# Results in a used-up operand, an earlier operand load, and four moved steps in an attention and squared-ReLU kernel

## The chip, the cores and the metric

The kernel runs on one core of one Trainium2 chip. The metric is device time in microseconds (us). The engines are named as in the profile: PE is TensorE (PEld its weight load), DVE is VectorE, ACT is ScalarE, POOL is GpSimd and SP is SyncE. SP and ACT issue the DMAs here; a "q" behind an engine's name (SPq, ACTq) marks its sequencer.

## The reference

Attention in which a query sees only keys of its own cluster, then a feed-forward block with a squared ReLU. There are 4 batches, 8 heads, 768 positions and 64 elements to a head; d_model is 512 and d_ff 2048. Everything is float32.

```
q_assign = argmax(normalized q . normalized centroids)      # 16 clusters to a head
k_assign = argmax(normalized k . normalized centroids)
scores   = where(q_assign == k_assign, q @ k.T / 8, -1e9)
x        = softmax(scores) @ v                              # (3072, 512)
h        = x @ w_in                                         # (3072, 2048)
out      = max(h, 0)**2 @ w_out                             # (3072, 512)
```

## The kernel before

**Attention.** The loop over `p` takes the 16 pairs of heads (`NG`), four to a batch. A pair has nine tiles of scores, keys along the partitions: six of the first 512 queries and three of the other 256. `tile_of(p, i)` does one: matmuls of mask rows (`mask`, L450) and of keys and queries (`score`, L441) into one PSUM tile of a pool of three, then the exponential on ACT (L457). DVE adds the exponentials up (`total`, L460), PE multiplies them with v (`times_v`, L475), and ACT copies the result to `xT` (L484). Transposed q and k come by a DMA transpose (`turn_words`, `qkT`). `logits` (L329) are products with the centroids, of a later pair, into the pool of score tiles; `number` turns them on DVE into mask rows, which come back by way of DRAM (`far`, `rows`).

The sums of the exponentials: `add_up` (L494) sums over partitions on PE into half of a score tile, `invert` (L503 to L509) transposes and inverts them on DVE and stores them in DRAM, `spread` (L516) loads them broadcast, and `finish` (L526) multiplies a pair's `xT` with them in two DVE operations. All of pair p-1 but `add_up` happens in pass p; the last pair's is done inside the first up stage.

**Feed-forward.** The batches go in the order 1, 2, 3, 0 (`FEED`; n counts them). Each has an up stage (times w_in, squares) and a down stage (times w_out). The products are done by Winograd's form of Strassen's scheme: seven products of half-size blocks instead of eight, with sums of blocks made ahead and results added up behind. `x_sums` makes four sums of the input on DVE (L538), one at each `next`; `w_sums` makes those of w_in on POOL. An up stage has eight groups (`F2`). A group's seven products (L767) go into PSUM banks, which rotate among six; ACT copies the first (L730), DVE adds the others (L724, L538), ACT and DVE take the squares. In the first up stage DVE also rounds the blocks of w_out that are still being loaded (`Rounding.between`, L145 to L153, three a group in six groups) and makes sums of w_out (`w_out_sum`). What follows a group is in `Rounding.behind(i)`: after i = 0 the last pair's `add_up`, `invert` and `spread`; after i = 2 its `finish` and the store of x of batch 3 to DRAM (`x_far`, L1184).

**The down stages.** Two thirds of a batch's rows (`TWO`, 256 columns of g) go through its own down stage with the scheme applied twice. The last thirds (`THIRD`) of two batches are kept in DRAM (`g_far`) and done together: the stages of n = 1 and n = 3 have fourteen units (of, j), `of` 0 for the batch itself and 1 for the two thirds, j the outer product; the stage of n = 2 has seven. A unit (`Down.run`) has seven inner products (L956) into the banks `one` and `two`; ACT copies the first (L1089); `parts` makes the sums of the next unit's left operand; `combine`, a generator in two halves, adds up the unit before (L833) and lists finished quarters of the output; `store` issues these on ACT's queue at the next unit (L1071). The order of the units is

```
(0,1) (0,4) (1,4) (1,1) (0,5) (1,5) (0,7) (1,7) (0,6) (1,6) (0,2) (1,2) (0,3) (1,3)
```

`load_right(j)` (L915) loads four sums of w_out for the next j, `load_left(j)` (L994) the thirds from `g_far` in four DMAs, and `LATER` says after which unit (1, j) which left operand is loaded. The results of a stage stand in spare places: g's own last third (`third`), the tiles of the input's sums (`x_t1`, `x_t2`, `x_t4`) and the output pool. Left operand 3 of `of` = 1 is loaded into the last third of the half h = 1 of g, where results 21 and 22 stand until they are stored. Left operand 4 of `of` = 0 is `g[:, 8:16, 1, 0:256]`, used only in the second unit.

The order on each engine is the order in which the code issues (`manual_schedule`), but for the first down stage, which a planner orders. DMAs take turns on eight completion semaphores. At the end all engines read a flag (L1222) and branch past a general path (L1235).

Of the kernel before, what the change touches and what calls it, by code (L numbers as in the profile page):

```python
# [8 lines left out]
F32 = mybir.dt.float32  # L9
# [9 lines left out]
P = 128  # L19
# [6 lines left out]
def kernel(  # L26
# [432 lines left out]
    def add(eng, out, a, b):  # L459
        eng.tensor_tensor(out=out, in0=a, in1=b, op=ALU.add)  # L460
# [51 lines left out]
    def spread(pair):  # L512
        far = reciprocals.pop(pair)
        rb = endp.tile([P, 2, 32, NBL], F32, name="rb")
        for e in range(2):
            nc.sync.dma_start(  # L516
                rb[D * e : D * (e + 1)].rearrange("p g i b -> p (g i b)"),
                far[e].rearrange("i b -> (i b)").partition_broadcast(D),
            )
        spread_out[pair] = rb  # L520

    def finish(pair):
        b, hp = divmod(pair, HP)
        x = x_of(b)[:, hp].rearrange("p (g b i) -> p g b i", g=2, b=NBL)
        for g in range(2):
            nc.vector.scalar_tensor_tensor(  # L526
                out=x[:, g], in0=x[:, g], scalar=UP,
                in1=spread_out[pair][:, g].rearrange("p i b -> p b i"),
                op0=ALU.mult, op1=ALU.mult,
            )  # L530
        spread_out.pop(pair)
# [32 lines left out]
    def tile_of(pair, i):  # L564
        begin(i)
        for j in range(len(spots(i))):
            mask(pair, i, j, True)
            score(pair, i, j, False)
        exponential(i)
# [21 lines left out]

    first_sums = []
    x_early, w_early = x_sums(FEED[0]), []
    for p in range(NG):
        if p == 0:
            load_qk(3)
            load_ahead(0)
        if p == HP + 1:
            nc.sync.dma_start(x_far[FEED[3]], xT.pop(FEED[3]))
        if p:  # L600
            invert(p - 1)
            turn_words(p + 2)
            spread(p - 1)
        if 2 < p + 1 < NG:
            turn_logits(p + 1)
            number(p + 1)
        load_v(p + 1)
        if p:
            load_ahead(p - 1)


        if p == 0:
            for i in range(2):
                turn(1, i, (V, M)[i])
                score(p, i, 0, True)
            turn_onehot()
            for t in rows_of:
                nc.vector.memset(t, 0.0)
            turn(1, 2, V)
            for i in range(NB):  # L620
                if i == 2:
                    begin(i)
                    score(p, i, 0, True)
                mask(p, i, 0, False)
                exponential(i)
        else:
            for i in range(NB):
                tile_of(p, i)
        total[p] = endp.tile([P, 2, S], F32, name="total")
        first, last = total[p][:, :, 0:QA], total[p][:, :, QA:S]  # L630
        add(nc.vector, first, ex[0], ex[1])
        if p < 2:
            logits(p + 1, begin("ls"))
            turn_logits(p + 1)
            number(p + 1)
        add(nc.vector, first, first, ex[2])
        for i in range(NB, NCH):
            tile_of(p, i)
            add(nc.vector, first, first, ex[i])
        if p == 0:  # L640
            for i in range(2):
                split_words(2, i, nc.scalar)
            turn_words(2)
        else:
            split_words(p + 3, 0)


        for i in range(NCH, NCH + NB):
            tile_of(p, i)
        part = accp.tile([P, 2, 512], F32, name="part")  # L650
        add(nc.vector, part, ex[NCH], ex[NCH + 1])
        add(nc.vector, part, part, ex[NCH + 2])
        add(nc.vector, last, part[:, :, 0:QB], part[:, :, QB : 2 * QB])
        if p:
            finish(p - 1)
            round_2(p - 1)
            round_3(p - 1)
        if p == 0:
            split_words(3, 0)
        split_words(p + 3, 1)  # L660
        load_qk(p + 4, (nc.scalar, nc.scalar))
        round_1(p)


        for i in range(NCH):
            times_v(p, i, V)
        evict(p, 0, V)
        for i in range(NCH, NCH + NB):
            times_v(p, i, M)
        raw_v.pop(p)  # L670
        if p + 1 < NG:
            bank = begin("ls")
            if 2 < p + 2:
                if p + 2 < NG:
                    logits(p + 2, bank)
            add_up(p, bank[:, 1])
        evict(p, NCH, M)
        for d in (qkT, ohT):
            d.pop(p)
        if p >= NG - 2:  # L680
            for _ in range(2):
                if (found := next(x_early)) is not None:
                    first_sums.append(found)
            w_early.append(w_sums(len(w_early)))
    att.close()

# [272 lines left out]

    LATER = {1: 7, 5: 6, 7: 2, 2: 3}
    LOADS = ({1: (0,), 2: (1,), 3: (2,), 4: (3,)}, {9: (0,), 10: (1, 2), 12: (3,)})

    class Down:
# [55 lines left out]
        def find_results(self):  # L1021
            def four(t):
                return t.rearrange("p (i n) -> p i n", i=4)

            def tile(pool, tag):
                return four(pool.tile([P, 4 * P], F32, name="c", tag=tag))

            third = [self.g[:, F4 * i : F4 * (i + 1), 1, THIRD] for i in range(3)]
            if self.n % 2:
                self.c = [  # L1030
                    {11: tile(tp, "x_t2"), 21: third[0], 22: third[2]},
                    {11: tile(tp, "x_t4"), 21: tile(tp, "x_t1"), 22: third[1]},
                ]
                self.extra = xp.tile([P, 3, F2, P], F32, name="extra", tag="x1")
            else:
                self.c = [dict(zip((11, 22, 21), third))]
            for c in self.c:
                c[12] = tile(outp, "osb")


        def combine(self, of, j, one, two, copied):
            c = self.c[of]
            r = c[{1: 11, 4: 21, 5: 12, 7: 22}[j]] if j in (1, 4, 5, 7) else four_r
            plus(r[:, 0:2], two[:, 0:2], copied.unsqueeze(1).to_broadcast([P, 2, P]))
            plus(r[:, 2], two[:, 2], r[:, 1])
            plus(r[:, 1:4:2], two[:, 3].unsqueeze(1).to_broadcast([P, 2, P]), r[:, 1:3])
            yield
            if j in (2, 3):
                to = c[{2: 11, 3: 12}[j]]
                plus(to, to, r)  # L1050
                plus(to[:, 1:3], one[:, 1:3], to[:, 1:3])
            else:
                plus(r[:, 1:3], one[:, 1:3], r[:, 1:3])
            if j == 7:
                sub(c[21], c[22], c[21])
            elif j == 6:
                plus(r, c[11], r)
                for to in (21, 12):
                    plus(c[to], c[to], r)
                plus(c[22], c[22], c[12])  # L1060
            for to in {6: (21, 22), 2: (11,), 3: (12,)}.get(j, ()):
                self.stores.append((of, to))

        def store(self, queues=(nc.scalar, nc.scalar)):
            for of, to in self.stores:
                h, m = divmod(to, 10)
                h, m = h - 1, m - 1
                cols = slice(M2 * m, M2 * (m + 1))
                for i in range(2):
                    b, block = (FEED[self.n - 1 + i], 2) if of else (self.b, i)  # L1070
                    queues[i].dma_start(  # L1071
                        out_view[b, NB * h + block][:, cols].rearrange("p (m n) -> p m n", m=2),
                        self.c[of][to][:, 2 * i : 2 * i + 2],
                    )
            self.stores = []

        def run(self):
# [3 lines left out]
            for u, (of, j) in enumerate(self.units):  # L1081
# [14 lines left out]
                if waiting:  # L1096
                    next(waiting)
                sub(x[0][1], x[0][1], s[:, 1])
                times(one[:, 1], x[0][1], y[1][1])
                if u + 1 < len(self.units):  # L1100
                    if (k := self.units[u + 1][1]) != j:
                        load_right(k)
# [13 lines left out]
                        self.load_left(5)  # L1116
                if waiting:
                    next(waiting, None)
                waiting = self.combine(of, j, one, two, copied)
                to_end = len(self.units) - 1 - u  # L1120
                for kk in LOADS[self.n % 2].get(u, ()):
                    load_x(self.n + 1, kk)
# [3 lines left out]
                    sum_x(self.n + 1, 2)  # L1126
            list(waiting)
            sum_x(self.n + 1, 1)
            self.store((nc.sync, nc.scalar) if self.n == B - 1 else (nc.scalar, nc.scalar))


    flag = const.tile([P, 1], I32, name="flag")
# [15 lines left out]
    class Rounding:  # L1148
# [27 lines left out]
        def behind(self, i):  # L1176
            nonlocal wtp, spare_tile, four_r
            if i == 0:
                add_up(NG - 1, bank_tile(TB))
                invert(NG - 1)  # L1180
                spread(NG - 1)
            if i == 2:
                finish(NG - 1)
                nc.sync.dma_start(x_far[FEED[2]], xT.pop(FEED[2]))  # L1184
            if i == 5:
# [238 lines left out]
```

## Time and profile before

| | us |
|---|---|
| median of 3 runs | 891.62 |
| lowest and highest | 891.22, 892.13 |
| profiled execution, its own time | 892.71 |
| its span, first to last instruction | 890.8 |

| engine | busy us | share of the span |
|---|---|---|
| PE | 877.4 | 98% |
| PEld | 584.9 | 66% |
| DVE | 703.6 | 79% |
| ACT | 389.9 | 44% |
| POOL | 146.1 | 16% |

The granted TensorE clock was 0.998 over the span. In a line of the timeline the first number is the start in us, the second the time taken by the x instructions of the line, and brackets hold the idle time of the engine before it and what ended that. In a list of waits the numbers are the total in us, how many, and the longest. In an answer on one source line the numbers behind the count are the shortest, median and longest duration in ns, and then the first and last start in us.

### The profile page before, as it was taken

The page shows a single profiled execution, that of the slowest core. Times are in us where ns is not written, and L with a number is a line of the kernel's source. Part 1 is how long each engine was busy: PE and PEld are TensorE (multiplying, and loading weights), DVE is VectorE, ACT ScalarE, POOL GpSimd, SP SyncE. Part 2 cuts the span into 40 slices and gives each one's busy share as a digit, 9 for nine tenths or more (in the row PEclk, how much of TensorE's full clock was granted, in tenths as well). Part 3 has the DMA queues.
Part 4 walks back from the last instruction along what each step waited for, and adds up shares of the span by engine and source line. Part 5 has one row for each costly group of instructions (what it writes and reads, how often), then busy time and mean ns, then how long its engine had stood idle before and what let it go on. Part 6 is the DMA issues. An engine that isn't in the chain of part 4 may idle for free.

```text
span 890.8 us, 14588 instructions
## 1 busy us (share of the span) xinstructions
PE 877.4 (98%) x5379; PEld 584.9 (66%) x5379; DVE 703.6 (79%) x1271; ACT 389.9 (44%) x621; POOL 146.1 (16%) x168
## 2 busy tenths in 40 slices
PE   9999999999999999999999999999999999999995
PEld 6444444444444555568855599996558975579995
DVE  6798888888888989999756686778568786586794
ACT  5877667777666657740045410003452025430000
POOL 0000100000000247720222200013320052300000
PEclk9999999999999999999999999999999999999999
DMA  7767787767754235326701165573113741127553
GB/s 249 180 182 207 217 246 193 197 178 214 211 148 115 85 142 173 129 67 232 282 33 48 41 187 188 162 240 104 51 53 124 227 148 48 41 92 240 159 151 121
DMA packets 165729, 136.04 MB, mean 153 GB/s; under 512 B 58794, under 2 KB 139282, under 8 KB 165394
## 3 DMA queue, kind: packets, MB, share of 16 engines
q1 hardware_dynamic: 149634, 119.78, 45.1%
q10 hardware_dynamic: 16016, 15.24, 5.4%
q8 instruction: 45, 0.74, 0.3%
q14 instruction: 34, 0.28, 0.1%
HBM read 82.10 MB, written 41.89 MB: 139 GB/s over the span
## 4 chain that ended last, share of the span: by engine, by line
PE 86%; DVE 8%; DMA 4%; issue 2%; ACT 1%; ACTq 0%; DVEq 0%; SPq 0%
PE bank L767 30%; PE bank L956 19%; PE sc L441 12%; PE av_a L475 8%; PE bank L848 5%; PE av_b L475 4%; PE sc L450 3%; DMA g<-g_far 1%; PE sc L329 1%; PE sc L494 1%; DMA qkT<-words 1%; DVE spare L833 1%; DVE g L724 1%; DVE c L833 1%; DVE g L538 1%
## 5 line engine op out<-in xcount | busy, mean ns | idle before, releaser
L457 ACT ACTIVATE ex<-sc 128x1024 f32<-128x1024 f32 x144 | 144.2, 1025 | 38.7 <-PE sc L441 32.0
L724 DVE TENSOR_TENSOR g<-bank,g 128x384 f32<-128x384 f32 x192 | 102.5, 552 | 71.8 <-PE bank L767 64.0
L441 PE MATMUL sc<-qkT 64*128 64x512 f32 (+1 forms) x768 | 150.5, 484 | 0.0
L743 ACT ACTIVATE g<-g 128x384 f32<-128x384 f32 x122 | 63.3, 519 | 102.0 <-DVE g L724 97.9
L767 PE MATMUL bank<-xT,w_s 128*128 128x384 f32 x256 | 93.2, 487 | 0.9 <-DVE g L724 0.9
L441 PEld LDWEIGHTS sc<-qkT 64*128 64x128 f32 x768 | 65.9, 188 | 41.9 <-issue 30.1
L767 PE MATMUL bank<-xT,w_in 128*128 128x384 f32 x256 | 93.2, 487 | 0.0
L767 PE MATMUL bank<-x_t,w_s 128*128 128x384 f32 x256 | 93.0, 486 | 0.0
L1089 ACT COPY spare<-bank 128x128 f32<-128x128 f32 x35 | 9.2, 263 | 189.7 <-PE bank L956 171.7
L475 PE MATMUL av_a<-ex,v_raw 128*64 128x512 f32 x384 | 85.9, 596 | 0.0
L460 DVE TENSOR_TENSOR total<-total,ex 128x1024 f32<-128x1024 f32 x64 | 78.7, 1229 | 6.5
L558 POOL TENSOR_TENSOR w_s<-w_in 128x256 f32<-128x256 f32 x32 | 26.0, 811 | 317.7 <-PE bank L956 145.6
L956 PE MATMUL bank<-home,l 128*128 128x128 f32 x560 | 74.1, 275 | 0.0
L767 PEld LDWEIGHTS bank<-xT,w_s 128*128 128x128 f32 x256 | 48.5, 190 | 35.4 <-issue 2.0
L767 PEld LDWEIGHTS bank<-x_t,w_s 128*128 128x128 f32 x256 | 48.6, 190 | 33.9 <-issue 0.2
L161 POOL TENSOR_TENSOR w_in<-w_in,w_raw 128x512 int32<-128x512 int32 x16 | 22.0, 1378 | 295.5 <-DVE w_in L153 295.5
L767 PEld LDWEIGHTS bank<-xT,w_in 128*128 128x128 f32 x256 | 48.3, 190 | 33.7 <-DVE g L538 0.6
L956 PEld LDWEIGHTS bank<-home,l 128*128 128x128 f32 x560 | 68.2, 192 | 0.1
L744 ACT ACTIVATE g<-g 128x384 f32<-128x384 f32 x122 | 63.8, 523 | 3.9
L475 PEld LDWEIGHTS av_a<-ex,v_raw 128*64 128x64 f32 x384 | 26.1, 137 | 51.0 <-issue 50.3
L450 PE MATMUL sc<-rows 64*128 64x512 bf16 (+1 forms) x360 | 59.0, 323 | 0.3 <-DVE sums_t L503 0.3
L767 PE MATMUL bank<-x_t,w_in 128*128 128x384 f32 x128 | 46.5, 486 | 0.0
(192 smaller groups left out, 1410.3 us busy)
## 6 DMA issues: line engine op xcount, KB each, us to landing
home<-w_far SPq DMA_DIRECT2D x92, 256.0 KB
words<-flat SPq DMA_DIRECT2D x26, 384.0 KB
w_raw<-in_moe_w_in_dram SPq DMA_DIRECT2D x16, 512.0 KB
w_raw<-in_moe_w_out_dram SPq DMA_DIRECT2D x16, 512.0 KB
w_far<-home SPq DMA_DIRECT2D x28, 256.0 KB
g<-g_far SPq DMA_DIRECT2D x28, 256.0 KB
v_raw<-in_v_dram SPq DMA_DIRECT2D x16, 384.0 KB
rb<-far_r SPq DMA_DIRECT2D x32, 192.0 KB
```

Source lines behind the costliest of these rows:

```text
L441: nc.tensor.matmul(sc[i][:, e, cols], lhsT=qkT[pair][rows, NCH + c], rhs=qkT[pair][rows, n.start // P : n.stop // P], start=first, stop=no ...
L450: nc.tensor.matmul(sc[i][:, e, cols], lhsT=ohT[pair][rows, 1, c * P : (c + 1) * P], rhs=ohT[pair][rows, 0, columns(i)], start=first, stop= ...
L457: nc.scalar.activation(out=ex[i], in_=sc.pop(i), func=ACT.Exp, scale=SCALE)
L460: eng.tensor_tensor(out=out, in0=a, in1=b, op=ALU.add)
L475: nc.tensor.matmul(bank[D * e : D * (e + 1), 0 : n.stop - n.start], lhsT=raw_v[pair][:, e, c], rhs=ex[i][:, e, cols], start=c == 0, stop=c ...
L558: nc.gpsimd.tensor_tensor(out=s1, in0=a[1][0], in1=a[1][1], op=ALU.add)
L724: nc.vector.tensor_tensor(out=out, in0=bank, in1=to, op=ALU.add)
L743: nc.scalar.activation(out=to, in_=to, func=ACT.Relu)
L744: nc.scalar.square(to, to)
L767: nc.tensor.matmul(bank, lhsT=operands[j][0][:, kk], rhs=operands[j][1][:, kk], start=(kk == 0), stop=(kk == H2 - 1),)
L848: nc.tensor.matmul(bank, lhsT=left[j][:, f], rhs=right(j)[:, f], start=(f == 0), stop=(f == F2 - 1),)
L956: nc.tensor.matmul(bank, lhsT=left[:, f], rhs=rhs[:, f], start=(f == 0), stop=(f == F4 - 1))
```

## The change

There are five edits.

- In the fourteen-unit down stages results 21 and 22 of both `of` stand in the place of left operand 4, `g[:, 8:16, 1, 0:256]`, and no longer in the last third or in `x_t1`. Left operand 3 is loaded after unit (1, 6) instead of (1, 2).
- The last pair's `spread` writes two tiles of the output pool with four DMAs (`spread_last`), instead of the tile `rb` with two. Its `finish` and the store of x of batch 3 stand after the seventh up group (i = 6) instead of the third.
- The first two sums of `x_sums` for batch 1 stand in the last pass, behind `invert` of pair 14, instead of at the end of the pass before it.
- In pass 1 the fourth score tile stands ahead of the logits of pair 2 instead of behind them.
- In the last unit of all the last inner product goes to a bank of its own; the addition that took two blocks takes one at a time, and each half of the last quarter is stored right after its addition, the first on SP's queue, the second on ACT's. The quarter of the unit before, which was stored on both queues ahead of this, is stored behind it, on ACT's queue.

```diff
-        spread_out[pair] = rb
+        spread_out[pair] = [rb[:, g] for g in range(2)]
+
+    def spread_last(pair):
+        far = reciprocals.pop(pair)
+        spread_out[pair] = []
+        for g in range(2):
+            rb = outp.tile([P, DM], F32, name="rb_last", tag="osb")[:, 0:TB]
+            for e in range(2):
+                nc.sync.dma_start(
+                    rb[D * e : D * (e + 1)],
+                    far[e, 32 * g : 32 * (g + 1)].rearrange("i b -> (i b)").partition_broadcast(D),
+                )
+            spread_out[pair].append(rb.rearrange("p (i b) -> p i b", i=32))
...
+    def early_x_sums():
+        for _ in range(2):
+            if (found := next(x_early)) is not None:
+                first_sums.append(found)
+
     for p in range(NG):
...
             invert(p - 1)
+            if p == NG - 1:
+                early_x_sums()
             turn_words(p + 2)
             spread(p - 1)
...
+        if p == 1:
+            tile_of(p, NB)
         if p < 2:
             logits(p + 1, begin("ls"))
...
         for i in range(NB, NCH):
-            tile_of(p, i)
+            if p != 1 or i > NB:
+                tile_of(p, i)
             add(nc.vector, first, first, ex[i])
...
         if p >= NG - 2:
-            for _ in range(2):
-                if (found := next(x_early)) is not None:
-                    first_sums.append(found)
+            if p == NG - 1:
+                early_x_sums()
             w_early.append(w_sums(len(w_early)))
...
-    LATER = {1: 7, 5: 6, 7: 2, 2: 3}
+    LATER = {1: 7, 5: 6, 7: 2, 6: 3}
...
-            third = [self.g[:, F4 * i : F4 * (i + 1), 1, THIRD] for i in range(3)]
+            def at(i, cols):
+                return self.g[:, F4 * i : F4 * (i + 1), 1, cols]
+
             if self.n % 2:
                 self.c = [
-                    {11: tile(tp, "x_t2"), 21: third[0], 22: third[2]},
-                    {11: tile(tp, "x_t4"), 21: tile(tp, "x_t1"), 22: third[1]},
+                    {
+                        11: tile(tp, f"x_t{2 * of + 2}"), 21: at(2, slice(P * of, P * (of + 1))),
+                        22: at(3, slice(P * of, P * (of + 1))),
+                    }
+                    for of in range(2)
                 ]
...
             else:
-                self.c = [dict(zip((11, 22, 21), third))]
+                self.c = [{to: at(i, THIRD) for i, to in enumerate((11, 22, 21))}]
...
-        def combine(self, of, j, one, two, copied):
+        def combine(self, of, j, one, two, copied, last=None):
...
                 plus(to, to, r)
-                plus(to[:, 1:3], one[:, 1:3], to[:, 1:3])
+                if last is None:
+                    plus(to[:, 1:3], one[:, 1:3], to[:, 1:3])
+                else:
+                    plus(to[:, 2], one[:, 2], to[:, 2])
+                    self.store_block(of, 12, 1, nc.sync)
+                    plus(to[:, 1], last, to[:, 1])
+                    self.store_block(of, 12, 0, nc.scalar)
+                    return
...
-        def store(self, queues=(nc.scalar, nc.scalar)):
+        def store(self):
             for of, to in self.stores:
...
+                for i in range(2):
+                    self.store_block(of, to, i, nc.scalar)
             self.stores = []
...
-                times(one[:, 1], x[0][1], y[1][1])
+                last = None
+                if self.n == B - 1 and u + 1 == len(self.units):
+                    last = bank_tile(P)
+                times(one[:, 1] if last is None else last, x[0][1], y[1][1])
...
-            self.store((nc.sync, nc.scalar) if self.n == B - 1 else (nc.scalar, nc.scalar))
+            self.store()
...
                 invert(NG - 1)
-                spread(NG - 1)
-            if i == 2:
+                spread_last(NG - 1)
+            if i == F2 - 2:
                 finish(NG - 1)
                 nc.sync.dma_start(x_far[FEED[2]], xT.pop(FEED[2]))
```

`store_block` holds the DMA that `store` issued before, for one half of a quarter on a given queue.

More of the change, by code (lines that the diff above doesn't have):

```diff
@@ L527, in finish @@
                 out=x[:, g], in0=x[:, g], scalar=UP,
-                in1=spread_out[pair][:, g].rearrange("p i b -> p b i"),
+                in1=spread_out[pair][g].rearrange("p i b -> p b i"),
                 op0=ALU.mult, op1=ALU.mult,
@@ L1062, in combine, with store_block @@
                 self.stores.append((of, to))
-        def store(self, queues=(nc.scalar, nc.scalar)):
+        def store_block(self, of, to, i, queue):
+            h, m = divmod(to, 10)
+            h, m = h - 1, m - 1
+            cols = slice(M2 * m, M2 * (m + 1))
+            b, block = (FEED[self.n - 1 + i], 2) if of else (self.b, i)
+            queue.dma_start(
+                out_view[b, NB * h + block][:, cols].rearrange("p (m n) -> p m n", m=2),
+                self.c[of][to][:, 2 * i : 2 * i + 2],
+            )
+        def store(self):
             for of, to in self.stores:
-                h, m = divmod(to, 10)
-                h, m = h - 1, m - 1
-                cols = slice(M2 * m, M2 * (m + 1))
                 for i in range(2):
[L1070 to L1074, printed above, removed]
+                    self.store_block(of, to, i, nc.scalar)
             self.stores = []
@@ L1118, in run @@
                     next(waiting, None)
-                waiting = self.combine(of, j, one, two, copied)
+                waiting = self.combine(of, j, one, two, copied, last)
                 to_end = len(self.units) - 1 - u
```

## The prediction

> **What bounds the kernel now.** I read the page first, then the waits of PE, then the timeline around each of those waits, then the lines on which the program ends.
>
> ```profile
> span 890.8 us, 14588 instructions
> PE 877.4 (98%) x5379; PEld 584.9 (66%) x5379; DVE 703.6 (79%) x1271; ACT 389.9 (44%) x621; POOL 146.1 (16%) x168
> ```
>
> PE is busy nearly always. No matmul is added or taken away, so only PE's idle time can be won: that between matmuls, and the 8.3 us between the last matmul (882.6) and the end. The waits of PE (total, times, longest) list nearly all of the first kind:
>
> ```profile
> PE bank L956 <- DMA g<-g_far: 1.7, 2, 1.3
> PE bank L767 <- DVE g L724: 0.9, 2, 0.6
> PE sc L329 <- DMA qkT<-words: 0.7, 1, 0.7
> PE bank L956 <- DVE g L538: 0.4, 1, 0.4
> PE sc L450 <- DVE sums_t L503: 0.3, 1, 0.3
> ```
>
> A stopped PE also restarts late, so I cost each wait by the delay of the following group against its usual spacing. The timeline shows the end of the last down stage:
>
> ```profile
> 868.08 2.63 SPq L994 DMA_DIRECT2D g<-g_far  x4
> 874.62 1.06 PE L956 MATMUL bank<-w_out,g 128*128 128x128 f32 x8
> 876.26 0.69 DVE L833 TENSOR_TENSOR l<-g 128x512 f32<-128x512 f32 x1 [5.22 <-DMA g<-g_far]
> 876.98 1.13 PE L956 MATMUL bank<-w_out,g 128*128 128x128 f32 x8 [1.30 <-DMA g<-g_far]
> 881.52 1.06 PE L956 MATMUL bank<-w_out,g 128*128 128x128 f32 x8
> 883.27 0.69 DVE L833 TENSOR_TENSOR c<-c,spare 128x512 f32<-128x512 f32 x1
> 884.07 0.42 DVE L833 TENSOR_TENSOR c<-bank,c 128x256 f32<-128x256 f32 x1
> ```
>
> The left operand of the last unit is requested at 868.08 and used at 876.26. DVE stands 5.22 us, PE 1.30. From 876.26 to 884.49 DVE works without rest and sets the end; PE had finished 1.9 us earlier. Line 1235, the closing branch, and the barrier behind it:
>
> ```profile
> L1235 SPq EVENT_SEMAPHORE  x8: 17/17/17, 888.9 to 889.5; - x8
> L1235 SPq COMPARE_BRANCH  x1: 58/58/58, 884.9 to 884.9; - x1
> L1235 ACTq COMPARE_BRANCH  x1: 54/54/54, 885.5 to 885.5; - x1
> L1235 ACTq EVENT_SEMAPHORE  x1: 17/17/17, 889.0 to 889.0; - x1
> L1419 POOLq EVENT_SEMAPHORE  x4: 17/17/17, 890.1 to 890.7; - x4
> ```
>
> SP branches at 884.9 after its last store and runs again only at 888.9; ACT needs 3.5 us for the same. SP then checks semaphores until 890.1, so ACT, there at 889.1, has 1.0 us to spare.
>
> **The change part by part.**
>
> *Logits of pair 2 behind tile 3 of pair 1.*
>
> ```profile
> 37.60 0.85 PE L329 MATMUL sc<-qkT,cnT 128*32 128x384 f32 x8 [0.66 <-DMA qkT<-words]
> 304.92 0.39 PE L450 MATMUL sc<-rows 64*128 64x512 bf16 x2 [0.26 <-DVE sums_t L503]
> 371.00 1.53 PE L767 MATMUL bank<-xT,w_s 128*128 128x384 f32 x4 [0.25 <-DVE g L724]
> 380.88 1.53 PE L767 MATMUL bank<-xT,w_s 128*128 128x384 f32 x4 [0.62 <-DVE g L724]
> ```
>
> Tiles start 1.075 us apart, so tile 3 could start at 36.79 and logits (0.78) at 37.87, after the transpose landed (37.5). Now tile 3 starts at 38.39 where 37.57 was possible: 0.82 won. Its bank is free: exponential 0 ended at 35.9. DVE gets the logits 0.3 us later, but the DMA that carries its marks away waits in SP's queue until 46.15 anyway. That leads to the mask rows of pair 2, whose last packet ended at 52.9; the first mask would want them at 53.7 instead of 54.5. Cover 0.8 us; without it up to 0.8 comes back. I take 0.82 (0 to 0.82).
>
> *Two input sums behind the inversion of pair 14.* They stand before it on DVE (301.47 to 304.3), and the score bank it frees is what the third tile waits for. Moved, the inversion runs as soon as its sums are ready and the tile starts at 304.50, not 304.92: 0.42 won. DVE's total is unchanged; what is late next are the sums themselves, about 0.8 us, and the group that reads the last of them runs 6 us later.
>
> *Last pair's scaling from the third to the seventh up group.* DVE is behind PE there:
>
> ```profile
> 352.16 2.71 DVE L526 SCALAR_TENSOR_TENSOR xT<-xT,rb 128x384 f32<-128x384 f32 x2
> ```
>
> Up groups are 9.03 us apart, but those ending in the 371.00 and 380.88 waits take 9.52 and 9.89: 0.49 + 0.86 = 1.35 lost. Without 2.7 us at 352, DVE meets the fifth group 1.2 to 1.5 us behind its matmuls, not 3.2, and no bank is late: 1.35 won (0.6 if half the lag builds up again). At the new place the group's DVE work is 7.8 us of PE's 9.03, so it has caught up. The pair's cost is 2.71 beside a POOL addition, and 1.61 at 298.42 without one. The Trainium skill, "SBUF — State Buffer", "SBUF: two separate sides", states that a DVE operation with two SBUF inputs and a POOL operation lock each other out whole; POOL's last sum ends at 386.1 and the scaling comes at about 386.3, so I take 1.6. By the rule DVE enters the eighth group about 1.4 us behind, by the row 2.5; both are less than the 3.2 that just stops PE, so neither costs. The new spreading issues four DMAs for two, about 1.1 us more on SP ahead of a weight load that is used 8 us later. The store of x moves past six weight loads, which it no longer delays; it goes out at about 388 and needs 6.5 us (354.93 to 361.4), and its space is overwritten from 402: nothing.
>
> *Results in the used-up operand, left operand 3 fetched two units earlier.* The four DMAs take 8.2 us (868.08 to 876.26). After the right operand's loads they can go at about 855.6 and land by 864, needed at 871: cover 7 us. On SP they pass the next right operand's loads (due 865) and, in the second down stage, three x loads (2.0 us later, used 20 us later). The stores of that unit on ACT may wait for a completion slot behind them, under 1 us, with the next copy 4 us off. One result more lies in the tile with 512 B pieces, so two stores (0.39 and 0.48 instead of 0.35 and 0.45 to issue) have smaller packets; nobody waits for them. In the second down stage PE loses 0.59 at 598.8 and 0.57 at 604.1: 1.16 won. In the last, 1.47 (876.98 instead of 875.51) and with it DVE's late run. Laid out anew on the same durations: last two-bank group complete 879.3; three additions to 880.5; the 128x512 one to 881.25.
>
> *Last stores.* The last product gets a bank of its own, so the addition before it needn't wait for it; six banks rotate and that one was read out about 7 us before: nothing. The 128x256 addition (0.42) becomes two of 128x128 (0.29 each, 0.33 apart): DVE ends at 881.95, not 881.7, so 2.54 earlier than 884.49. SP's one last store goes out at 881.6. But the two stores of the unit before, until now issued at 882.15 on both queues, follow the last one on ACT's queue: three issues of 0.37, then 0.45 to 1.35 each (second of a pair: 0.45 at 869.52, 1.35 at 879.38). ACT is done at 883.4 (to 885.1), plus 0.53 load, branch and 3.5: ready 887.6 against 889.1. SP is through at 887.3 against 890.1. The barrier opens about 0.1 behind the later: 887.7 to 889.2 against 890.1. By the rule of "DMA: Bandwidth & Descriptors" in the skill ("Anatomy of one DMA"), a fixed cost of about 2.0 us per DMA, the end would move with the last issue: 884.52 to 882.95, 1.6 won. The trace speaks for the branch: 3.9 us pass on SP after the last issue whatever lands. I take 2.0 with PE's 1.47 inside it (0.9 to 2.6).
>
> Sum: 0.82 + 0.42 + 1.35 + 1.16 + 2.0 = 5.75. The profiled execution took 892.71 (span 890.8); it would take 886.96. The median lies 1.09 below it: 885.9.
>
> **The rivals.** *Half of it comes back* (0.20): the mask rows hold pair 2 (0), DVE's lag stops PE once more (0.6), a slow ACT issue (1.2). With 0.42 and 1.16: 3.4 won, 888.2. For it: the 1.35 us issue. Against: the covers above.
>
> *The load is no earlier* (0.07): results and load destination are interleaved columns of one tile; if the load waits for the whole tile, both down-stage waits stay and the end pays 0.4 for the stores: 0.82 + 0.42 + 1.35 - 0.4 = 2.2, 889.4. Against: other loads go into that tile beside reads of it without a wait.
>
> *Slower* (0.05): the x store now stands just before the first down stage, and DVE writes its space at 402. Everything on DVE queues behind that write, among it the additions at 416.5 that free banks; PE wants one at 419.4, so 2.9 us are covered. A landing after 405 costs PE one for one; after about 412 the kernel is slower than before. At 415 it would be 885.9 + 10 = 896. Against: 6.5 us in the trace, from 388.
>
> **How the numbers follow.** A change of about 0.2% (1.8 us) is what a measurement of this kernel can tell from none. The forecast has 0.64 and its own range is 885 to 887; with the first rival the range of 884.8 to 888.9 holds a little over 8 in 10. What is left (0.04) is an unseen wait that takes about all. Faster: 0.64 + 0.20 + half of the 0.07, 0.88; same: the other half and most of the rest, 0.06; slower 0.06.
>
> **What would show it.** The waits of PE have no g_far row, no qkT row, no L724 row; L526's last pair stands at about 386 and takes 1.6; the rows of L994 for operand 3 come two units earlier. The last DVE addition ends 5 to 6.5 us earlier than 884.5, ACT issues three stores behind it, and ACT, not SP, is last at the barrier. A new PE wait between 395 and 444, or on L450 near 53, would prove me wrong.

## The result and the profile after

| | before | after |
|---|---|---|
| median of 6 runs, us | 891.42 | 885.93 |
| lowest and highest, us | 890.65, 892.13 | 885.41, 886.99 |
| profiled execution, us | 892.71 | 885.83 |
| its span, us | 890.8 | 884.0 |

The ratio is 0.994 with a 95% interval of 0.9928 to 0.9953: 5.5 us faster. Line numbers have moved: L956 of before is L979, L767 is L790, L724 is L747, L833 is L856, L538 is L551, L526 is L539, L994 is L1017, L1071 is L1104, the branch at L1235 is L1276, and the barrier at L1419 is L1460. Some experiments have these lines a few numbers off.

Two lines of the page after, in the form of those shown of before:

```profile
span 884.0 us, 14579 instructions
...
PE 876.0 (99%) x5379; PEld 584.3 (66%) x5379; DVE 702.7 (79%) x1272; ACT 390.2 (44%) x621; POOL 145.5 (16%) x168
```

The waits of PE that the view lists for the changed kernel (total us, times, longest):

```profile
PE sc L179 <- DVE zeros L176: 1.1, 1, 1.1
PE av_a L274 <- DMA q_raw<-in_q_dram: 0.4, 1, 0.4
```

Only the two waits of the first four microseconds are left; all five rows shown of before are gone. The logits of pair 2, the third tile of the last pair, the seventh up group (its product at the place of the wait at 380.88 of before), the scaling, and then the last unit in the timeline:

```profile
37.98 0.85 PE L329 MATMUL sc<-qkT,cnT 128*32 128x384 f32 x8
...
303.80 0.38 PE L450 MATMUL sc<-rows 64*128 64x512 bf16 x2
...
377.19 1.45 PE L790 MATMUL bank<-xT,w_in 128*128 128x384 f32 x4
378.61 1.53 PE L790 MATMUL bank<-xT,w_s 128*128 128x384 f32 x4
379.98 1.45 PE L790 MATMUL bank<-x_t,w_s 128*128 128x384 f32 x4
...
387.23 1.59 DVE L539 SCALAR_TENSOR_TENSOR xT<-xT,rb_last 128x384 f32<-128x384 f32 x2
...
851.98 2.08 SPq L1017 DMA_DIRECT2D g<-g_far  x4
...
867.40 0.69 DVE L856 TENSOR_TENSOR l<-g 128x512 f32<-128x512 f32 x1
...
873.05 0.69 DVE L551 TENSOR_TENSOR g<-g,l 128x512 f32<-128x512 f32 x1 [1.46 <-PE bank L979]
...
877.84 0.49 DVE L856 TENSOR_TENSOR c<-bank,c 128x128 f32<-128x128 f32 x2
```

The first two have no bracket any more. The product at 378.61 has none either, but it starts 1.42 us behind the one ahead of it, and the next 1.37 us behind it, where the usual spacing is 1.29: about 0.2 us are still lost there, too little at once for the list. The scaling takes 1.59 us where it took 2.71. Left operand 3 is requested at 851.98 and first read at 867.40, with no wait on either engine. In the last unit the roles are turned: DVE waits for PE (1.46 us), and its two last additions end at 878.33, 0.85 us behind PE's last product (877.48) where it was 1.92. The closing branch and the barrier:

```profile
L1276 SPq EVENT_SEMAPHORE  x8: 17/17/17, 881.7 to 882.3; - x8
L1276 SPq COMPARE_BRANCH  x1: 58/58/58, 878.5 to 878.5; - x1
L1276 ACTq COMPARE_BRANCH  x1: 54/54/54, 880.4 to 880.4; - x1
L1276 ACTq EVENT_SEMAPHORE  x1: 17/17/17, 883.2 to 883.2; - x1
L1460 POOLq EVENT_SEMAPHORE  x4: 17/17/17, 883.3 to 883.9; - x4
```

SP's eight checks pass without a stop; ACT, with three stores behind DVE's end, arrives at 883.2, and the barrier opens right behind it.

### The profile page after: what moved, and what is told of

It is laid out like the page before. It is cut to its first block, busy times and chain, and to the rows that moved or that the text cites. A ratio compares the mean times of both kernels' runs of the same rounds, so it can differ in the third digit from the quotient of the medians.

```text
span 884.0 us, 14579 instructions
## 1 busy us (share of the span) xinstructions
PE 876.0 (99%) x5379; PEld 584.3 (66%) x5379; DVE 702.7 (79%) x1272; ACT 390.2 (44%) x621; POOL 145.5 (16%) x168
## 4 chain that ended last, share of the span: by engine, by line
## 5 line engine op out<-in xcount | busy, mean ns | idle before, releaser
L747 DVE TENSOR_TENSOR g<-bank,g 128x384 f32<-128x384 f32 x192 | 102.5, 552 | 73.2 <-PE bank L790 67.8
L790 PE MATMUL bank<-xT,w_in 128*128 128x384 f32 x256 | 93.2, 487 | 0.0
L790 PE MATMUL bank<-xT,w_s 128*128 128x384 f32 x256 | 93.1, 486 | 0.0
L790 PE MATMUL bank<-x_t,w_s 128*128 128x384 f32 x256 | 93.0, 486 | 0.0
L979 PE MATMUL bank<-home,l 128*128 128x128 f32 x560 | 74.0, 275 | 0.0
L790 PEld LDWEIGHTS bank<-xT,w_s 128*128 128x128 f32 x256 | 48.6, 190 | 34.2 <-issue 0.6
L790 PEld LDWEIGHTS bank<-x_t,w_s 128*128 128x128 f32 x256 | 48.6, 190 | 33.9
L790 PEld LDWEIGHTS bank<-xT,w_in 128*128 128x128 f32 x256 | 48.3, 190 | 33.7 <-DVE g L551 0.6
L979 PEld LDWEIGHTS bank<-home,l 128*128 128x128 f32 x560 | 68.2, 192 | 0.1
L767 ACT ACTIVATE g<-g 128x384 f32<-128x384 f32 x122 | 63.8, 523 | 3.9
L790 PE MATMUL bank<-x_t,w_in 128*128 128x384 f32 x128 | 46.5, 486 | 0.0
```

Of the source, the lines that this page charges most:

```text
L747: nc.vector.tensor_tensor(out=out, in0=bank, in1=to, op=ALU.add)
L767: nc.scalar.square(to, to)
L790: nc.tensor.matmul(bank, lhsT=operands[j][0][:, kk], rhs=operands[j][1][:, kk], start=(kk == 0), stop=(kk == H2 - 1),)
L979: nc.tensor.matmul(bank, lhsT=left[:, f], rhs=rhs[:, f], start=(f == 0), stop=(f == F4 - 1))
```

## The experiments

The totals of two executions differ by more than single edits are worth, so each kernel is read by stretches of one profile of it, worked out from the starts of PE's groups. *Attention* is from the first logits to the first product of the first up stage; *first up* is that stage; *n = 1* and *n = 3* are the fourteen-unit down stages (the last up to PE's end); *DVE* is how far its end lies behind PE's; *rest* is from there to the last instruction. All in us, with the ratio to before.

| kernel | attention | first up | n = 1 | n = 3 | DVE | rest | ratio (95%) |
|---|---|---|---|---|---|---|---|
| before | 312.25 | 74.67 | 89.02 | 89.24 | 1.92 | 6.34 | |
| changed | 311.08 | 73.54 | 87.74 | 87.71 | 0.85 | 5.72 | 0.994 (0.9928 to 0.9953) |
| a0, the changed again | 311.08 | 73.55 | 87.55 | 88.21 | 0.85 | 6.07 | 0.9947 (0.9933 to 0.996) |
| x1, late load | 311.08 | 73.52 | 89.04 | 88.46 | 1.66 | 5.88 | 0.9974 (0.9965 to 0.9984) |
| x2, scaling in third group | 311.08 | 74.77 | 87.54 | 87.71 | 0.84 | 6.25 | 0.9965 (0.9954 to 0.9977) |
| x3, stores ahead | 311.08 | 73.59 | 87.68 | 87.80 | 0.85 | 5.36 | 0.9934 (0.9921 to 0.9948) |
| x3b, the same again | 311.08 | 73.49 | 88.13 | 87.71 | 0.84 | 5.57 | 0.9937 (0.9921 to 0.9953) |
| x4, old last stores | 311.08 | 73.53 | 88.03 | 87.71 | 0.79 | 5.75 | 0.9939 (0.9925 to 0.9952) |
| x5, logits first | 311.70 | 73.53 | 87.75 | 87.71 | 0.85 | 6.25 | 0.9961 (0.9948 to 0.9974) |
| x6, sums first | 311.52 | 73.37 | 87.55 | 87.71 | 0.85 | 6.42 | 0.9956 (0.9943 to 0.9969) |
| x7, places and load alone | 311.85 | 74.63 | 87.59 | 87.71 | 0.78 | 5.64 | 0.9969 (0.9957 to 0.9981) |
| x8, load a unit later | 311.08 | 73.48 | 88.56 | 87.71 | 0.84 | 5.38 | 0.9943 (0.9926 to 0.996) |
| x9, last stores alone | 311.78 | 74.64 | 89.18 | 88.26 | 1.77 | 6.40 | 0.9998 (0.9988 to 1.0008) |

**The changed kernel again (a0).**

> The changed kernel once more, as the mark for the others. My account of its gain: PE loses 5.1 us less (0.72 logits, 0.42 sums, 1.13 scaling, 1.28 and 1.53 in the two fourteen-unit down stages), DVE ends 1.07 us closer behind PE, and the span's last part, from DVE's end to the last instruction, which fell from 6.35 to 5.71 in the profile, differs only because the closing branch's fetch took 2.8 us on ACT instead of 3.5. If that is chance, this profile shows another value there, between 5.5 and 7, and the gain over before is 5 to 6 us (ratio 0.9935 to 0.9945). Rival: the last part is really shorter through the edit of the stores; then it is 5.7 again to within 0.1.

886.86 us, 4.3 less than before on the same chip (891.12): less than the 5 to 6 that I had written, with a ratio just outside the range given. The rest is 6.07, in the range that chance was given, but the 5.72 had another cause than a lucky branch. One row of the barrier tells it:

```profile
L1276 SPq EVENT_SEMAPHORE  x8: 17/17/17, 882.6 to 883.9; - x8
```

SP's eight checks take 1.3 us here, not 0.6. In the trace SP stands 0.8 us at the check of the semaphore that ACT's third store counts; that store was issued at 880.09, so it landed 3.7 us later. SP, not ACT, was last. In the changed kernel's first profile the trace has the third store (issued at 879.24) landed at 881.85, after 2.6 us, and SP found it done.

**The load late again (x1).**

```diff
-    LATER = {1: 7, 5: 6, 7: 2, 6: 3}
+    LATER = {1: 7, 5: 6, 7: 2, 2: 3}
```

> The results stay in the used-up operand, left operand 3 is loaded after unit (1, 2) again. Theory (the earlier load is what pays): PE waits for g_far at the end of both fourteen-unit stages again, 1.2 to 1.5 us each with the late sums behind it, DVE ends about 1.9 us behind PE instead of 0.85: 3.5 to 4 us slower than the changed kernel, so about 1.7 us faster than before. Rival (the freed places pay, since the load need not wait for stores of results out of its destination): the load, issued at the same unit, lands about 2 us sooner and most of the gain stays, less than 1.5 us slower than the changed kernel.

889.33 us, 2.5 us slower than a0, between the two forecasts. Waits of PE and a line of DVE's timeline:

```profile
PE bank L979 <- DMA g<-g_far: 0.5, 1, 0.5
PE bank L979 <- DVE g L551: 0.5, 1, 0.5
```

```profile
873.38 0.69 DVE L856 TENSOR_TENSOR l<-g 128x512 f32<-128x512 f32 x1 [4.12 <-DMA g<-g_far]
```

With the places alone the stage of n = 1 is as long as before (89.04), and DVE again waits 4 us in n = 3 and ends late (1.66). So the earlier load is what pays. The rival also fails in x9, which has the old places: its late load was used 6.4 and 6.7 us after its request, x1's 6.8 and 7.1, so freed places do not make a late load land sooner. That the early load needs the new places follows from the code, since results 21 and 22 stood where it lands; no run tried it without them. That less came back than I wrote lies in n = 3: the load was used 7.1 us after its request (866.25 to 873.38), not 8.2. x9 lost only 0.55 there too, so before's profile shows a slow instance of that wait.

**The scaling behind the third group (x2).**

```diff
-            if i == F2 - 2:
+            if i == 2:
```

> The changed kernel with the last pair's scaling and the store of x behind the third up group again (the spreading by four DMAs into two tiles stays). Theory (DVE's lag is what stops PE): the pair of operations takes 2.7 us beside POOL instead of 1.6, DVE is about 3 us behind PE in the fifth group, and PE waits for L747's bank twice; the first up stage takes 1.1 to 1.35 us longer, and the time rises as much. Rival (the six weight loads that wait behind the store of x cause the lag): the same waits, but ACT's first operation on w_out waits for the load at that place; with PE no later than in the changed kernel if neither holds.

First up is 1.2 us longer, and no other stage moves. Waits of PE, the scaling and the next idle time of DVE, and one line of ACT:

```profile
PE bank L790 <- DVE g L747: 1.0, 2, 0.6
```

```profile
350.62 2.71 DVE L539 SCALAR_TENSOR_TENSOR xT<-xT,rb_last 128x384 f32<-128x384 f32 x2
...
362.07 0.56 DVE L747 TENSOR_TENSOR g<-bank,g 128x384 f32<-128x384 f32 x1 [0.20 <-ACT g L753]
```

```profile
356.93 0.69 ACT L133 ACTIVATE w_out<-w_raw 128x512 f32<-128x512 f32 x1 [1.02 <-DMA w_raw<-in_moe_w_out_dram]
```

At this place the pair takes 2.71 us, as before; in the seventh group it took 1.59. The rival's sign appears as well: ACT waits 1.02 us for a block of w_out. But DVE works without idle time from 350.62 to 362.07, so this load did not hold DVE up, and ACT waits for DVE again at 360.98 (2.26 us). PE's two waits name DVE's additions. The theory stands.

**The logits first (x5) and the sums first (x6).**

```diff
-        if p == 1:
-            tile_of(p, NB)
...
-            if p != 1 or i > NB:
-                tile_of(p, i)
+            tile_of(p, i)
```

> The changed kernel with the logits of pair 2 ahead of the fourth tile again. Theory: PE waits 0.6 to 0.7 us for the transposed words at about 37 us, and everything behind it is 0.7 us later: +0.7 us. Rival: another wait later in the attention or DVE's work takes up the difference, and the first up stage starts less than 0.2 us later.

```diff
-            if p == NG - 1:
-                early_x_sums()
             turn_words(p + 2)
...
-            if p == NG - 1:
-                early_x_sums()
+            early_x_sums()
```

> The changed kernel with the two input sums ahead of the inversion again. Theory: PE waits 0.26 us at the third tile of the last pair and its tile starts 0.4 us later: +0.4 us, which the times alone can hardly tell. Rival: without DVE's other lag nothing waits there and the stages start at the same times.

One timeline row of each, x5 and then x6:

```profile
39.56 0.85 PE L329 MATMUL sc<-qkT,cnT 128*32 128x384 f32 x8 [0.54 <-DMA qkT<-words]
```

```profile
304.20 0.39 PE L450 MATMUL sc<-rows 64*128 64x512 bf16 x2 [0.27 <-DVE sums_t L503]
```

Attention is 0.62 and 0.44 us longer than the 311.08 that eight executions with both edits share to the hundredth, and x5's difference reaches the stages behind it whole. Of x6's only 0.27 do: its first up stage is 0.17 shorter, because PE, coming later, loses 0.04 us at the place in the seventh group where the changed kernel loses 0.2. Both theories hold, though DVE's lag takes up over a third of x6's difference. The profiled execution of x5 (889.00 us) says little, as its attention began 2 us late (below).

The wait for the transposed words has no fixed size. It was 0.66 us before and 0.54 in x5, but only 0.25 and 0.19 in x7 and x9, which have the logits first too:

```profile
36.41 0.85 PE L329 MATMUL sc<-qkT,cnT 128*32 128x384 f32 x8 [0.19 <-DMA qkT<-words]
```

Their attention is 0.3 us longer than x6's, where the table has 0.7 for before. So the edit of the logits is worth 0.3 to 0.7 us, and before's profile shows a slow instance here as well.

**Places and load alone on the kernel before (x7).**

> The kernel before with the new places of the results and the earlier load alone. Theory (the edits do not need each other): the two down stages get shorter by 1.3 and 1.5 us, DVE ends 0.85 us behind PE: 3.5 to 4 us faster than before. Rival (part of this needs the earlier stages' timing): less than 3 us.

This is the first of the five edits made on the kernel before. 887.57 us against 890.55, a ratio of 0.9969: 2.8 us, just inside the rival's bound, with an interval of 1.7 to 3.8 us. The size forecast was missed, the mechanism was not: n = 1 (87.59) and n = 3 (87.71) are as short as in the changed kernel and DVE ends 0.78 us behind PE, so the edit does not need the others. That is 4.1 us less than in before's profile and 3.1 less than in x9's, whose load waited less; I had taken my 3.5 to 4 from the slower one.

**The last stores: ahead again (x3, x3b), undone (x4), and alone on before (x9).** In x3 and x3b the quarter of unit (0, 3) is stored as soon as it is ready:

```diff
                 if last is None:
                     plus(to[:, 1:3], one[:, 1:3], to[:, 1:3])
+                    if self.n == B - 1 and j == 3:
+                        self.store_block(of, 12, 0, nc.sync)
+                        self.store_block(of, 12, 1, nc.scalar)
+                        return
```

> The changed kernel with the quarter of the unit before the last stored ahead of the last stores again, one half on SP's and one on ACT's queue; one store each remains behind the last additions. Theory (the two stores queued behind the last one on ACT cost time): ACT reaches its closing branch 0.9 us earlier and the end comes 0.3 to 0.9 us earlier than in the changed kernel. Rival (the landing of the last store or SP's own path sets the end): the end moves by less than 0.2 us.

> The kernel of x3_stores_ahead once more, as the mark for the next one and to see whether its end repeats. Theory: from DVE's end to the last instruction about 5.4 us, against 5.7 to 6.4 in the runs with three stores behind DVE's end on ACT; SP, not ACT, is last at the barrier; the ratio to before is 0.993 to 0.9945. Rival: 5.4 us was a lucky fetch behind the branch; then it is 5.7 or more here.

x4 takes the edit back as a whole, and x9 makes it alone on the kernel before. The main lines of x4:

```diff
-                if self.n == B - 1 and u + 1 == len(self.units):
-                    last = bank_tile(P)
...
-            self.store()
+            self.store((nc.sync, nc.scalar) if self.n == B - 1 else (nc.scalar, nc.scalar))
```

> The changed kernel with the edit of the last stores undone as a whole: one 128x256 addition, then one store on SP and one on ACT, the quarter before stored ahead on both. Theory: DVE ends 0.2 us earlier than in the changed kernel, SP's last store goes out 0.1 us later and ACT's branch comes 1.0 us earlier: 0.2 to 0.8 us faster than the changed kernel, so this edit did not help. Rival (the early half store and the bank of its own pay): slower by 0.1 to 0.5 us.

> The kernel before with the edit of the last stores alone. DVE is the late engine at the end there, and PE's last product lies 2 us back, so its own bank can bring nothing. Theory: DVE ends 0.2 us later behind PE, ACT issues three stores behind it and comes to its branch about 1 us later, being last at the barrier: the same to 0.6 us slower than before. Rival: the earlier half store pays and it is 0.2 us or more faster.

SP's checks and ACT's arrival in x9, then in x3b:

```profile
L1248 SPq EVENT_SEMAPHORE  x8: 17/17/17, 885.6 to 887.3; - x8
...
L1248 ACTq EVENT_SEMAPHORE  x1: 17/17/17, 887.1 to 887.1; - x1
```

```profile
L1280 SPq EVENT_SEMAPHORE  x8: 17/17/17, 882.8 to 883.4; - x8
...
L1280 ACTq EVENT_SEMAPHORE  x1: 17/17/17, 883.5 to 883.5; - x1
```

x4 took 886.11 us, 0.75 less than a0. With three stores on ACT behind DVE's end, SP's checks took 1.1 to 1.7 us in six of seven profiles; with one they took 0.5 to 0.6 in all six. The rest is 6.1 on average over those seven, 5.4 in x3, x3b and x8, and 5.7 in x4 and x7, where DVE ends 0.06 earlier. So the halved addition and the early half store are worth about 0.2 us, and the two stores that were put behind take 0.7. As a whole the edit of the last stores is 0.4 to 0.5 us against the change, as far as two profiles with the old stores tell; before's own, with a rest of 6.34, is left out of this for its slow return from the branch (below). The times of x9 (0.9998, 0.9988 to 1.0008) show neither gain nor loss, and two details of its forecast failed: SP, not ACT, was last, and DVE's end was not later. In x4 DVE's end was 0.06 us earlier, not 0.2. x3 and x3b came as forecast; that x3b's rest is 0.2 longer than x3's is the branch (3.4 us on SP instead of 3.2). I had explained x3 by ACT's branch alone. That is about half of it: the one profile with three stores in which no check stopped SP has a rest of 5.72, midway between x3's 5.36 and a0's 6.07.

**The load a unit later (x8).**

```diff
                     if of and j in LATER:
                         self.load_left(LATER[j])
+                    if self.n % 2 and (of, j) == (0, 2):
+                        self.load_left(3)
```

The kernel is x3, with `6: 3` also taken out of `LATER`.

> x3_stores_ahead with left operand 3 loaded after unit (0, 2) instead of (1, 6), one unit nearer to its use. In one profile of the changed kernel PE waited 0.26 us for the right operand's last block at 857 us, which shares its landing with the 1 MB of the left operand and the stores. Theory (that wait comes from the crowding behind unit (1, 6)): no PE wait on home in unit (0, 2), stage lengths of 87.5 to 87.7 us and 87.7 us. Rival (the later load crowds the next right operand instead, or lands too late for the last unit's sums): PE waits on home in unit (0, 3) or DVE waits for g_far, and the stages are 0.3 to 1 us longer. In the times under 0.5 us either way.

PE's waits have one row more than x3b's:

```profile
PE bank L979 <- DVE home L551: 0.8, 1, 0.8
```

It stands at 591.62, before the first product of unit (0, 3) that reads a loaded block of right operand 3. The DVE operation named ends at 591.58, but x3b's PE starts this product while that operation is running (PE at 591.35, DVE from 591.24 to 591.93), so the product does not need it. What PE waited for is the block: requested at 585.51 behind 1 MB of the left operand and two x loads, it landed at 591.49, 0.13 us before PE went on. In x3b it landed at 591.22, again 0.13 before PE. n = 1 is 0.4 to 1.0 us longer than in the other kernels with the early load, n = 3 the same. The rival holds for one of two stages. By these profiles unit (1, 6) is the better place (the times, 886.52 us against x3b's 885.77, overlap), but not free: in a0's n = 3 PE waited 0.26 us for `home<-w_far`, and x4 and x3b had 0.14 and 0.15 at 591 in n = 1. These stages are 0.3 to 0.5 us longer than their likes.

**A version that is probably better than the changed kernel** is x3: 885.33 us where a0 had 886.86 on the same chip, ranges apart, though 0.4 us of this, by the profiles, is a0's wait in n = 3. x3b had 885.77 on another chip. The intervals of the ratios overlap (0.9934 and 0.9937 against 0.994 and 0.9947), so the times alone do not decide; the profiles show 0.7 us less in the rest on average.

## Why the prediction was right

The time forecast was 885.9, measured 885.93. The waits and what ends them were forecast rightly, but what sets the very end was not. That the time fits to 0.03 us is luck: the sum was 0.3 larger than the difference of the medians, before's median came out 0.2 lower with six runs than with three, and the same kernel took 886.86 when run again. Term by term, in us:

| step | forecast | profile before to after | undone or alone |
|---|---|---|---|
| logits behind the fourth tile | 0.82 | 0.72 | 0.62 (x5), 0.3 against x7 and x9 |
| sums behind the inversion | 0.42 | 0.42 | 0.44 (x6), 0.27 net |
| scaling in the seventh group | 1.35 | 1.13 | 1.2 (x2) |
| down stage of n = 1 | 1.16 | 1.28 | 1.3 to 1.5 (x1) |
| down stage of n = 3 and the end | 2.0 | 1.53 + 1.07 + 0.62 = 3.2 | |

- *Where PE waits.* All five waits left the list, each for the reason given. The covers held: the mask rows did not stop pair 2, no wait came up between 395 and 444, and the scaling took 1.59 us at 387.23, forecast 1.6 at 386. The rule from the Trainium skill ("SBUF — State Buffer", "SBUF: two separate sides"), that such a DVE operation and a POOL operation lock each other out, agrees with the traces: in x2 the second operation of the pair took 1.95 us while POOL made an addition of 1.84 us, the first 0.84; in the seventh group, with no POOL operation beside them, both took 0.83. The logits term was 0.1 too large, since logits start 1.17 us behind the tile ahead of them and not 1.075, in all nine profiles with this edit alike; the words had landed half a microsecond before (37.41, used at 37.98). The scaling's was 0.2 too large: "no bank is late" did not hold, as the seventh group took 9.24 us and not 9.03.
- *DVE's late run.* DVE was to end 2.54 us earlier for the last stage alone; it ended 1.53 + 1.07 = 2.60 earlier.
- *The step that was mis-sized is the rest of the end.* I let it grow by 0.54 (2.0 in all, with 2.54 from DVE's end). Between the two profiles it fell by 0.62. That is not the edit's doing: SP's return from the branch took 3.94 us in before's profile, but 3.24 and 3.35 in x7 and x4, which have the same last stores. Against those two the edit costs 0.4 on average, close to the 0.54, but by another road. I said that what lands behind the branch doesn't matter, and set ACT's branch against the landing of the last store. With SP back after 3.0 to 3.1 us and the third store landed 3.5 to 4.0 us after its issue in the six profiles where SP stood for it, SP waits for the landing. The 2.0 us that I took from the skill's "DMA: Bandwidth & Descriptors" are given there, under "Anatomy of one DMA", for DMAs that GpSimd issues; ACT issued these, and the third of three in a row took longer. But that the landing counts was the reading to keep: it decides in those six, and ACT's arrival in the changed kernel's own profile, where the forecast of ACT as the last was right.
- *Span and median.* The spans differ by 6.8 us, the medians by 5.5, and by 4.3 when run again (a0). Before's profiled execution lies 1.3 above its median of six runs, the other 0.1 below. I had set my sum against 892.71 and taken 1.09 off. This execution was slow in three of the things that I costed: the wait for the words (0.66 against 0.19 to 0.54 elsewhere), the load in n = 3 (1.53 against 0.55 in x9) and the branch (0.6).
- *The rivals.* None of the three came as a whole. Two traces of the first did: DVE's lag still costs 0.2 us in the seventh group, and right operands that land later beside the earlier load cost 0.3 to 0.5 us in three of the eighteen fourteen-unit stages with the load after (1, 6).

## What to carry to other kernels

When an engine is 98% busy, list its few waits and cost each by the delay of the group behind it; five waits under 1.5 us made 5 us here, and they added up nearly whole, because PE had little other idle time behind them to take them up. Take the size of a wait for a DMA from more than one profile: one such wait was 0.66 us here in one execution and 0.19 in another. A load that must wait for results to leave its destination is helped by giving those results another place, if it is then also asked for earlier: the place alone left both waits here (x1). At the end of a program put as few stores as possible behind the last computation, and ask of each both when its queue gets free and when it lands.

## What the runs showed of the hardware

- *The start.* The first logits began between 7.5 us (x9) and 10.3 us (x5) after the first instruction, with the same code before them. This moves the whole execution. Behind it the stages that no edit touches agree between all 13 profiles to 0.01 us: 48.66 or 48.67 for the first down stage, 43.77 for that of n = 2.
- *The return from a taken branch* took 3.0 to 3.9 us on SP and 2.7 to 3.5 us on ACT over 13 profiles, so it is no constant. On SP it was 3.04 to 3.13 us in all seven profiles with three stores on ACT behind DVE's end and 3.16 to 3.94 in the six others. So a part of it may go with the stores; why is not shown.
- *Three 128 KB stores in a row on ACT's queue* took 0.34, 0.46 and 0.47 us to issue, as forecast at the lower end, but the last landed 3.5 to 4.0 us after its issue in the six profiles where SP stood for it, and 2.6 us after it in the seventh.
